# A retention layer and two dense layers on one core: third and fourth head pairs crossed, all loads on one queue, two w_in halves decoded beside the tiles

## The chip, the core and the metric

The kernel runs on one core of one Trainium2 chip. The metric is device time in microseconds (us) from one launch to its end; lower is better. The kernel before takes 866.6 us (median of 3 runs, 865.91 to 866.82).

## What is computed

Three steps follow one another. The reference, cut to what matters:

```python
# q, k, v: (4, 8, 576, 64): 4 batches, 8 heads, 576 positions, 64 wide
gamma = 1.0 - 2.0 ** (-5.0 - np.arange(8))
Dmat = np.where(rel >= 0, gamma[:, None, None] ** rel, 0.0)      # rel = i - j
x = ((q @ k.T) / 8 * Dmat) @ v                                   # -> (2304, 512)
h = x @ w_in;   g = relu(h) ** 2;                x = g @ w_out     # 512 -> 2048 -> 512
h = x @ w_in2;  g = h * clip(h + 3, 0, 6) / 6;   y = g @ w_out2
```

The four weight matrices arrive as 64-bit floats and are decoded to 32 bits on the chip; q, k and v are 32-bit.

## The kernel before

**The tile stage (first 82 us).** The positions of a batch are cut into four tiles of 128 and a last one of 64. There are 20 tiles in the order `tiles`: the tiles of batches 0 and 1 alternate (numbers 0 to 9), then those of batches 2 and 3 (10 to 19). So tiles 8, 9, 18 and 19 are the short last ones, and 0, 1, 10 and 11 the first of their batches. A tile needs two loads: `qkt` (keys and queries, 512 KB) and `kvt` (keys and values by position, 512 KB; in a short tile only the values, 64 rows of 2 KB that are wanted on both halves of the 128 partitions). There are five places for tiles (`TOKENS`), so the loads of tile t+5 wait until tile t is used up. Round ti of the loop issues on TensorE (PE) the scores of tile ti (`aps`), then for tile ti-1 the values (`vps`), the state sums (`sps`) and the queries (`vps` again, none in the first tile of a batch). VectorE (DVE) turns `aps` into `ret`, which `vps` needs, and `vps` into `xall`, the input of the next layer. ScalarE (ACT) copies the state, GpSimd (POOL) scales the keys of a tile (`scale_keys`).

**Weights beside the tiles.** One "half" is a 128-wide slice of one weight matrix, 512 KB as it arrives. `load_w` loads it into a tile `stage`; `decode` makes 32 bits of it in four steps: ACT (`first`), DVE (`clamp`, `second`, `third`). `halves` is the list of the order in which halves are loaded and decoded. Before, the loads number 1 to 7 are issued from ACT's queue, at the places where ACT comes to them, and all others from SP's queue; halves w_in 0, w_in 1 and w_out 0 are decoded between tiles 6 and 11.

**The first layer (82 to 476 us).** It goes over four groups of positions (`FIRST`); within one, 16 units c. A unit is `emit_h` (h = x w_in for 128 of the 2048 columns, banks `hps`), `emit_g` (ACT: relu, square, rounding to `g`; DVE: the remainder) and, two units later (`LAG`), `y_steps` (`yps`, `ytail`). `split_in` and `split_out` cut a decoded half into a high part (ACT copy) and a low part (a subtraction on the engine named) for products of three passes. In the first group `emit_h` writes the same two banks in each unit, so that unit c+1 can start only when ACT has read unit c out (`r<-hps`). Within a unit the engines work in the order of the code: what stands after a waiting instruction on its engine waits too.

**Order of the loads.** SP and ACT issue their loads in the order of the code. The built program has eight completion semaphores for loads and gives them to the loads of both queues in turn, so that each load also waits until the load eight places ahead in the code has landed.

**Crossed pairs.** A head pair a holds heads 2a and 2a+1, which lie on partitions 0 to 63 and 64 to 127. For pairs 1 and 3 `stage_values` writes the two heads to swapped halves, `constants` holds the matching decay (`crossed`), and `load_w` loads the rows of w_in for these two pairs with swapped halves:

## Time and profile before

| what | value |
|---|---|
| median of 3 runs | 866.6 us |
| the profiled execution: its time | 864.64 us |
| the profiled execution: its span, first to last instruction | 862.9 us |
| PE busy | 839.4 us, 97% of the span |
| DVE, ACT, POOL busy | 526.2, 459.5, 138.5 us |
| granted TensorE clock, mean | 0.990 |
| start of the first layer (first `hps`) | 81.65 us |
| chain that ended last | PE 82%, DMA 6%, issue 5%, ACT 3%, POOL 2%, DVE 2% |

The profiled execution took 1.74 us more than its span, and 1.96 us less than the median of the three runs. PE's share of 97% is an average: in the 40 slices of the profile its busy tenths stand at 8777999 in the first seven, and from the eighth on at 9 but for the last. The column PEclk has 8 or 9 in the same first slices.

### The profile page before, as it was taken

The page shows a single profiled execution, that of the slowest core. Times are in us where ns is not written, and L with a number is a line of the kernel's source. Part 1 is how long each engine was busy: PE and PEld are TensorE (multiplying, and loading weights), DVE is VectorE, ACT ScalarE, POOL GpSimd, SP SyncE. Part 2 cuts the span into 40 slices and gives each one's busy share as a digit, 9 for nine tenths or more (in the row PEclk, how much of TensorE's full clock was granted, in tenths as well). Part 3 has the DMA queues.
Part 4 walks back from the last instruction along what each step waited for, and adds up shares of the span by engine and source line. Part 5 has one row for each costly group of instructions (what it writes and reads, how often), then busy time and mean ns, then how long its engine had stood idle before and what let it go on. Part 6 is the DMA issues. An engine that isn't in the chain of part 4 may idle for free.

```text
span 862.9 us, 13373 instructions
## 1 busy us (share of the span) xinstructions
PE 839.4 (97%) x4962; PEld 728.3 (84%) x4962; DVE 526.2 (61%) x896; ACT 459.5 (53%) x878; POOL 138.5 (16%) x117
## 2 busy tenths in 40 slices
PE   8777999999999999999999999999999999999998
PEld 6676888888888888888888898888988988989886
DVE  5575677777476777787675645456554546643433
ACT  2323877677676777787765533335433345433332
POOL 3141333332133313432140000000000000000000
PEclk9889999999999999999999999999999999999999
DMA  9884265655577688778759445545565463774531
GB/s 342 282 302 143 98 187 185 186 196 180 194 288 271 227 285 287 271 266 295 262 202 333 167 159 213 189 151 179 191 268 200 159 217 113 262 259 162 178 115 73
DMA packets 67529, 184.21 MB, mean 213 GB/s; under 512 B 6536, under 2 KB 23048, under 8 KB 67464
## 3 DMA queue, kind: packets, MB, share of 16 engines
q1 hardware_dynamic: 63656, 178.54, 59.0%
q10 hardware_dynamic: 3808, 4.82, 1.7%
q8 instruction: 39, 0.64, 0.3%
q14 instruction: 26, 0.21, 0.1%
HBM read 147.16 MB, written 36.18 MB: 212 GB/s over the span
## 4 chain that ended last, share of the span: by engine, by line
PE 82%; DMA 6%; issue 5%; ACT 3%; POOL 2%; DVE 2%; SPq 0%; ACTq 0%; DVEq 0%; POOLq 0%
PE yps L574 23%; PE hps L608 20%; PE hps L390 18%; PE yps L433 17%; DMA kvt<-in_kv_dram 2%; DMA qkt<-in_qk_dram 2%; DMA stage<-in_w_in_dram 1%; PE ytail L433 1%; POOL win L186 1%; POOL wo L186 1%; PE vps L303 1%; PE aps L255 1%; ACT r L411 0%; DVE ret L263 0%; ACT r L162 0%
## 5 line engine op out<-in xcount | busy, mean ns | idle before, releaser
L574 PE MATMUL yps<-wo,g 128*128 128x512 f32 x864 | 226.3, 394 | 0.0
L433 PE MATMUL yps<-g,wo 128*128 128x512 f32 x768 | 195.7, 392 | 0.6 <-POOL wo L186 0.5
L574 PEld LDWEIGHTS yps<-wo,g 128*128 128x128 f32 x864 | 159.6, 188 | 23.6 <-DVE g L623 0.3
L433 PEld LDWEIGHTS yps<-g,wo 128*128 128x128 f32 x768 | 140.0, 188 | 28.5 <-POOL wo L186 4.1
L390 PE MATMUL hps<-xring,win 128*128 128x512 f32 (+1 forms) x720 | 154.8, 364 | 0.3 <-ACT r L410 0.3
L390 PEld LDWEIGHTS hps<-xring,win 128*128 128x128 f32 x720 | 124.1, 190 | 21.9 <-ACT r L410 0.5
L608 PE MATMUL hps<-xlast,win 128*128 128x384 f32 x576 | 116.1, 336 | 0.0
L608 PEld LDWEIGHTS hps<-xlast,win 128*128 128x128 f32 x576 | 103.2, 188 | 8.8
L627 DVE TENSOR_TENSOR u<-hps,u 128x384 f32<-128x384 f32 x48 | 26.7, 557 | 107.3 <-PE hps L608 107.3
L416 DVE TENSOR_TENSOR g<-r,g 128x512 fp32r<-128x512 f32 x64 | 47.5, 742 | 73.0 <-ACT g L412 72.6
L608 PE MATMUL hps<-xop,win 128*128 128x384 f32 x432 | 87.2, 336 | 0.0
L410 ACT ACTIVATE r<-hps 128x512 f32<-128x512 f32 x80 | 43.9, 549 | 75.9 <-PE hps L390 75.9
L608 PEld LDWEIGHTS hps<-xop,win 128*128 128x128 f32 x432 | 77.5, 188 | 6.6
L621 ACT ACTIVATE g<-c 128x384 fp32r<-128x384 f32 x72 | 37.8, 525 | 84.0 <-DVE c L620 84.0
L619 ACT ACTIVATE v<-c,three 128x384 f32<-128x384 f32 x72 | 44.4, 617 | 32.9 <-DVE c L627 31.7
L390 PE MATMUL hps<-xown,win 128*128 128x512 f32 x240 | 59.8, 390 | 0.7 <-ACT xall L442 0.7
L165 DVE TENSOR_SCALAR a<-a 128x512 f32<-128x512 f32 x64 | 38.5, 601 | 25.6 <-ACT a L161 25.6
L390 PEld LDWEIGHTS hps<-xown,win 128*128 128x128 f32 x240 | 44.8, 188 | 10.1 <-ACT xall L442 0.9
L185 ACT ACTIVATE win<-w 128x512 fp32r<-128x512 f32 x64 | 39.6, 620 | 25.2 <-DVE w L180 23.7
L646 ACT ACTIVATE c<-hps 128x384 f32<-128x384 f32 x24 | 11.8, 492 | 76.7 <-PE hps L608 76.7
L411 ACT ACTIVATE r<-r 128x512 f32<-128x512 f32 x80 | 47.2, 590 | 2.5
L620 DVE SCALAR_TENSOR_TENSOR c<-v,c 128x384 f32<-128x384 f32 x72 | 39.9, 555 | 13.7 <-ACT v L619 13.7
(77 smaller groups left out, 1000.4 us busy)
## 6 DMA issues: line engine op xcount, KB each, us to landing
wo<-kept SPq DMA_DIRECT2D x96, 512.0 KB, 5.3
win<-kept SPq DMA_DIRECT2D x72, 512.0 KB, 3.3
kept<-ready SPq DMA_DIRECT2D x40, 512.0 KB, 3.8
stage<-in_w_out_dram SPq DMA_DIRECT2D x30, 512.0 KB, 4.0
qkt<-in_qk_dram SPq DMA_DIRECT2D x16, 512.0 KB, 8.9
kvt<-in_kv_dram SPq DMA_DIRECT2D x16, 512.0 KB, 8.9
kept<-wo SPq DMA_DIRECT2D x16, 512.0 KB, 5.0
stage<-in_w_in_dram SPq DMA_DIRECT2D x16, 512.0 KB, 3.8
```

What stands on the lines that cost most here:

```text
L165: nc.vector.tensor_scalar(out=a, in0=a, scalar1=LEAST, scalar2=MOST, op0=ALU.max, op1=ALU.min)
L185: nc.scalar.activation(out=hi, in_=src, func=ACTF.Copy)
L390: nc.tensor.matmul(out=h, lhsT=w[:, wp, kk * 128:kk * 128 + 128], rhs=xs[pos, kk][xp][:, o:o + n], start=m == 0, stop=m == 3 * KD - 1,)
L410: nc.scalar.activation(out=r, in_=hs[k], func=ACTF.Relu)
L411: nc.scalar.activation(out=r, in_=r, func=ACTF.Square)
L416: nc.vector.tensor_tensor(out=lo, in0=src, in1=hi.bitcast(F32), op=ALU.subtract)
L433: nc.tensor.matmul(out=p, lhsT=w[:, wp, m * 128:m * 128 + 128], rhs=g[pos, c][k][:, gpart, :size], start=c == 0 and e == 0 and not (k and ...
L574: nc.tensor.matmul(out=p, lhsT=gt[m // 3][:, gpart, m % 3 * 128:][:, :128], rhs=w[:, wp], start=first and e == 0, stop=last and e == 2,)
L608: nc.tensor.matmul(out=to, lhsT=wl[k][:, half, wp, o], rhs=x[:, xp, f], start=first and m == 0, stop=last and m == 5, skip_group_check=True,)
L619: nc.scalar.activation(out=v, in_=c, func=ACTF.Relu, bias=three)
L620: nc.vector.scalar_tensor_tensor(out=c, in0=v, scalar=6.0, in1=c, op0=ALU.min, op1=ALU.mult)
L621: nc.scalar.activation(out=hi, in_=c, func=ACTF.Copy)
```

## The change

1. Pairs 2 and 3 are crossed instead of 1 and 3, and crossed in such a way that the rows of w_in for pair 2's place in `xall` are the 128 consecutive rows 320 to 447. `stage_values` and `stage_queries` write pairs 0 and 1 into one bank and pairs 2 and 3 into the other, and all loops over pairs go in the order 0, 2, 1, 3. The halves that consecutive products write are the same as before.
2. A w_in half comes by four loads (256, 128, 64 and 64 KB) instead of three (256, 128, 128 KB).
3. All halves are loaded from SP's queue; ACT issues none.
4. The values of a short tile come by two loads of 64 partitions instead of one load whose source repeats the rows (`twice`).
5. w_out 0 is no longer decoded beside the tiles. It is decoded in the first unit of the first layer, behind w_in 2, and the low part of its split is done by DVE and no longer by POOL. The two decodes that stay beside the tiles come two tiles later, the splits one tile later or earlier; w_in 0 and w_in 1 are loaded two tiles later.

`AHEAD` is used nowhere.

```diff
@@ constants
-    crossed[:, 1::2] = np.roll(pair, D, axis=0)[:, 1::2]
+    crossed[:64, 2:], crossed[64:, 2] = pair[64:, 2:], pair[:64, 3]
+    crossed[64:, 3] = pair[:64, 2]
@@ load_w
-        queue = nc.scalar if turn["stage"] <= 7 else nc.sync
...
-                queue.dma_start(out=t[:, ::2], in_=src[:, ::2])
-                for e in range(2):
-                    queue.dma_start(out=t[64 * e:64 * e + 64, 1::2], in_=src[64 - 64 * e:128 - 64 * e, 1::2])
+                nc.sync.dma_start(out=t[:, :2], in_=src[:, :2])
+                rows = w_in[:, c * 128:(c + 1) * 128]
+                nc.sync.dma_start(out=t[:, 2], in_=rows[320:448])
+                nc.sync.dma_start(out=t[:64, 3], in_=rows[448:])
+                nc.sync.dma_start(out=t[64:, 3], in_=rows[256:320])
...
-        queue.dma_start(out=t, in_=src)
+        nc.sync.dma_start(out=t, in_=src)
@@ load_kv
-            twice = kv[b, C * i:C * i + n, 1].unsqueeze(0).to_broadcast([2, n, H, D])
-            nc.sync.dma_start(out=kvt[:, 1], in_=twice)
+            for e in range(2):
+                nc.sync.dma_start(out=kvt[half(e), 1], in_=kv[b, C * i:C * i + n, 1])
@@ scale_keys and below
+    PAIRS = (0, 2, 1, 3)
+    def column(a, e):
+        return a % 2 if a < 2 else 1 - (a % 2 ^ e)
@@ stage_values
-        for a in range(HP):
+        for a in PAIRS:
             for e in range(2):
-                to = e ^ a % 2
                 nc.tensor.matmul(
-                    out=p[a % 2][64 * to:64 * to + 64, a // 2, :n],
+                    out=p[a // 2][half(e ^ a // 2), column(a, e), :n],
                     lhsT=kvt[keys(n, e), 1, 2 * a + e, :], rhs=r[keys(n, e), e, a, :n],
-                    start=a < 2, stop=i == 0, skip_group_check=True,
+                    start=a % 2 == 0, stop=i == 0, skip_group_check=True,
@@ halves
-    halves = [(-2, 0, 0, 0), (-2, 0, 1, 0), (-2, 0, 0, 1), (-1, 0, 2, 0)] + sorted(halves, key=lambda x: x[0])
+    halves = [(-2, 0, 0, 0), (-2, 0, 1, 0), (-1, 0, 2, 0), (-1, 0, 0, 1)] + sorted(halves, key=lambda x: x[0])
@@ loop over the tiles
-            if ti in (1, 3, 5) or ti >= len(tiles) - 4:
+            if ti in (3, 5) or ti >= len(tiles) - 5:
                 load()
-            if ti >= 6 and ti % 2 == 0 and halves[0][0] < -1:
+            if ti >= 8 and ti % 2 == 0 and halves[0][0] < -1:
...
-            if ti in (11, 13, 15, 17):
-                split_x(0, (ti - 11) // 2)
-            if ti in (14, 16):
-                split_in(0, (ti - 14) // 2, nc.gpsimd)
+            if ti in (12, 14, 16, 18):
+                split_x(0, (ti - 12) // 2)
+            if ti in (13, 15):
+                split_in(0, (ti - 13) // 2, nc.gpsimd)
@@ first layer
-        due = [decode(*halves.pop(0)[1:])]
-        due[0].pop(0)()
+        due = [decode(*halves.pop(0)[1:]) for _ in range(2)]
+        for d in due:
+            d.pop(0)()
...
-                split_out(max(i - 1, 0), nc.gpsimd)
+                split_out(max(i - 1, 0), nc.vector if i == 0 else nc.gpsimd)
```

**SP's queue around tiles 7 to 10.** These are SP's loads for tiles 7, 8, 9 and the first of tile 10 before; the rows of L227 are the repeated loads of the short tiles 8 and 9.

```order
L217 DMA qkt<-in_qk_dram 128x1024
L224 DMA kvt<-in_kv_dram 128x1024
L217 DMA qkt<-in_qk_last_dram 128x512
L227 DMA kvt<-in_kv_dram 128x1x512
L217 DMA qkt<-in_qk_last_dram 128x512
L227 DMA kvt<-in_kv_dram 128x1x512
L217 DMA qkt<-in_qk_dram 128x1024
```

The same place of the changed kernel, from the second load of tile 7 on:

```order
L226 DMA kvt<-in_kv_dram 128x1024
L135 DMA stage<-in_w_in_dram 128x2x128
L137 DMA stage<-in_w_in_dram 128x128
L138 DMA stage<-in_w_in_dram 64x128
L139 DMA stage<-in_w_in_dram 64x128
L219 DMA qkt<-in_qk_last_dram 128x512
L229 DMA kvt<-in_kv_dram 64x512 x2
L219 DMA qkt<-in_qk_last_dram 128x512
L229 DMA kvt<-in_kv_dram 64x512 x2
L135 DMA stage<-in_w_in_dram 128x2x128
L137 DMA stage<-in_w_in_dram 128x128
```

The loads of w_in 0 have moved in front of tile 8's, those of w_in 1 in front of tile 10's, and each repeated load has become two. The last five halves of the stage stand behind tile 19's loads now.

**ACT's queue in tiles 0 to 5.** Before, ACT's instructions from the first state copies on; L135, L137 and L141 are loads of halves that it issues.

```order
L289 ACTIVATE state<-sps,cst 128x64 x4
L135 DMA stage<-in_w_in_dram 128x2x128
L137 DMA stage<-in_w_in_dram 64x2x128 x2
L289 ACTIVATE state<-sps,cst 128x64 x8
L135 DMA stage<-in_w_in_dram 128x2x128
L137 DMA stage<-in_w_in_dram 64x2x128 x2
L289 ACTIVATE state<-sps,cst 128x64 x8
L141 DMA stage<-in_w_out_dram 128x512
```

In the changed kernel no load stands there: the state copies of tiles 0 to 7 follow one another, and then come the two decodes.

**DVE at the first unit.** Before, from the last `xall` of the tile stage on: the decode of w_in 2 (L165 to L180, its result is `w_1102`), then the remainders of `g`, and then the next decode.

```order
L323 TENSOR_TENSOR xall<-vps,cst 128x2x64 x4
L165 TENSOR_SCALAR a<-a 128x512
L168 TENSOR_SCALAR a<-a 128x512
L174 SCALAR_TENSOR_TENSOR a<-stage,a 128x512
L180 ISA w_1102<-a,r 128x1024
L416 TENSOR_TENSOR g<-r,g 128x512
L416 TENSOR_TENSOR gtail<-r,gtail 128x256
L165 TENSOR_SCALAR a<-a 128x512
```

The same place of the changed kernel; `wd` is the decoded w_out 0 and `wo` its split:

```order
L333 TENSOR_TENSOR xall<-vps,cst 128x2x64 x4
L167 TENSOR_SCALAR a<-a 128x512
L170 TENSOR_SCALAR a<-a 128x512
L176 SCALAR_TENSOR_TENSOR a<-stage,a 128x512
L182 ISA w_1102<-a,r 128x1024
L167 TENSOR_SCALAR a<-a 128x512
L170 TENSOR_SCALAR a<-a 128x512
L424 TENSOR_TENSOR g<-r,g 128x512
L424 TENSOR_TENSOR gtail<-r,gtail 128x256
L176 SCALAR_TENSOR_TENSOR a<-stage,a 128x512
L182 ISA wd<-a,r 128x1024
L188 TENSOR_TENSOR wo<-wd,wo 128x512
```

The second half of w_out 0's decode and the low part of its split now stand behind the remainders of the first unit's `g`. ACT's high part of that split waits for L182 `wd`, and it stands on ACT ahead of the next unit's `r<-hps`.

## Rows read from the trace of the kernel before

**Rows 1.** Windows: stretch, length, busy us (instructions) of PE, PEld, DVE, ACT, POOL, PEclk, DMA share, GB/s.
```profile
8.00:14.00 6.00, 4.80 (x88) 4.35 (x90) 5.22 (x11) 1.31 (x6) 3.13 (x3) 1.00 1.02 411
14.00:24.00 10.00, 8.41 (x170) 7.48 (x170) 5.37 (x11) 2.40 (x11) 2.09 (x2) 1.00 1.04 325
27.50:30.00 2.50, 2.50 (x24) 2.27 (x24) 0.72 (x2) 0.00 (x0) 0.49 (x1) 0.50 1.01 410
37.00:46.00 9.00, 3.27 (x96) 2.97 (x96) 6.41 (x15) 3.17 (x8) 0.00 (x0) 0.88 1.03 324
...
77.50:80.80 3.30, 0.00 (x0) 0.00 (x0) 1.00 (x4) 0.00 (x0) 0.00 (x0) 1.00 0.17 62
...
110.00:200.00 90.00, 89.92 (x511) 77.15 (x510) 67.16 (x105) 67.61 (x129) 30.10 (x22) 1.00 0.61 189
```

**Rows 2.** The chain that ended last, first 82 us: start, length, what.
```profile
21.25 5.81 DMA qkt<-in_qk_dram
...
33.19 13.47 DMA qkt<-in_qk_dram
...
66.66 14.13 DMA kvt<-in_kv_dram
```

**Rows 3.** Timeline of PE: start, length, what, count of matmul records, [idle before and what ended it].
```profile
17.47 1.16 PE L255 MATMUL aps<-qkt 64*128 64x128 f32 x16 [0.73 <-DMA qkt<-in_qk_dram]
...
21.58 1.16 PE L255 MATMUL aps<-qkt 64*128 64x128 f32 x16 [0.86 <-DVE xall L323]
...
27.20 2.08 PE L255 MATMUL aps<-qkt 64*128 64x128 f32 x16 [2.37 <-DMA qkt<-in_qk_dram]
...
33.03 1.41 PE L255 MATMUL aps<-qkt 64*128 64x128 f32 x16
...
46.79 2.08 PE L255 MATMUL aps<-qkt 64*128 64x128 f32 x16 [6.52 <-DMA qkt<-in_qk_dram]
...
55.38 1.16 PE L255 MATMUL aps<-qkt 64*128 64x128 f32 x16
...
62.90 1.16 PE L255 MATMUL aps<-qkt 64*128 64x128 f32 x16
...
66.08 1.16 PE L255 MATMUL aps<-qkt 64*128 64x128 f32 x16
...
80.92 0.46 PE L303 MATMUL vps<-ret,kvt 64*64 64x64 f32 x16 [3.70 <-DMA kvt<-in_kv_dram]
...
81.65 10.08 PE L390 MATMUL hps<-xring,win 128*128 128x512 f32 x48
92.04 4.45 PE L390 MATMUL hps<-xring,win 128*128 128x512 f32 x24 [0.31 <-ACT r L410]
```

**Rows 4.** Timeline of SP's queue: the repeated load of short tile 8.
```profile
25.76 0.69 SPq L227 DMA_DIRECT2D kvt<-in_kv_dram  x1
```

**Rows 5.** Timeline of DVE: tile 19's ret, unit 0's remainder, and two steps of a decode.
```profile
77.18 0.87 DVE L263 TENSOR_TENSOR ret<-aps,decay_last 64x256 f32<-64x256 f32 x2
...
89.35 0.43 DVE L416 TENSOR_TENSOR gtail<-r,gtail 128x256 fp32r<-128x256 f32 x1 [0.48 <-ACT gtail L412]
...
97.37 0.69 DVE L174 SCALAR_TENSOR_TENSOR a<-stage,a 128x512 int32<-128x512 int32 x1
98.20 0.69 DVE L180 CUSTOM_DVE_ANT_0 wd<-a,r 128x1024 uint16<-128x1024 uint16 x1
```

**Rows 6.** Waits of PE in the first 82 us: us in total, times, longest.
```profile
PE vps L303 <- DVE ret L263: 1.3, 3, 0.6
```

**Rows 7.** Timeline of POOL: the scaling of tile 3's keys, started by its load.
```profile
14.77 1.05 POOL L240 TENSOR_TENSOR kvt<-kvt,cst 128x512 f32<-128x512 f32 x1 [1.60 <-DMA kvt<-in_kv_dram]
```

**Rows 8.** Timeline of ACT: read-out of units 0 and 1, and between them w_out 0's split.
```profile
86.16 0.60 ACT L410 ACTIVATE r<-hps 128x512 f32<-128x512 f32 x1 [2.39 <-PE hps L390]
...
89.75 0.61 ACT L185 ACTIVATE wo<-wd 128x512 fp32r<-128x512 f32 x1
...
91.41 0.57 ACT L410 ACTIVATE r<-hps 128x512 f32<-128x512 f32 x1
```

More of the change, by code (lines that the diff above doesn't have):

```diff
@@ L36 @@
 LAG = 2
-AHEAD = 3
+AHEAD = 2
 WARM = 18
@@ L242, in scale_keys, with half @@
         )
+    def half(i):
+        return slice(64 * i, 64 * i + 64)
     def keys(n, e):
-        return slice(0, n) if n == C else slice(64 * e, 64 * e + 64)
+        return slice(0, n) if n == C else half(e)
+    PAIRS = (0, 2, 1, 3)
+    def column(a, e):
+        return a % 2 if a < 2 else 1 - (a % 2 ^ e)
     def stage_scores(ti):
@@ L256, in stage_scores @@
                     out=pe[e][keys(n, e), a, :n],
-                    lhsT=qkt[64 * e:64 * e + 64, 0, a, :n],
-                    rhs=qkt[64 * e:64 * e + 64, 1, a, :n],
+                    lhsT=qkt[half(e), 0, a, :n],
+                    rhs=qkt[half(e), 1, a, :n],
                     start=True, stop=True,
@@ L298, in stage_values @@
         p = [next_bank([128, 4, C], "vps") for j in range(2)]
-        for a in range(HP):
+        for a in PAIRS:
             for e in range(2):
-                to = e ^ a % 2
                 nc.tensor.matmul(
-                    out=p[a % 2][64 * to:64 * to + 64, a // 2, :n],
+                    out=p[a // 2][half(e ^ a // 2), column(a, e), :n],
                     lhsT=kvt[keys(n, e), 1, 2 * a + e, :], rhs=r[keys(n, e), e, a, :n],
-                    start=a < 2, stop=i == 0, skip_group_check=True,
+                    start=a % 2 == 0, stop=i == 0, skip_group_check=True,
                 )
@@ L312, in stage_queries @@
         qkt = data.pop(ti)[0]
-        for a in range(HP if i else 0):
+        for a in PAIRS if i else ():
             for e in range(2):
-                own, to = slice(64 * e, 64 * e + 64), e ^ a % 2
                 nc.tensor.matmul(
-                    out=p[a % 2][64 * to:64 * to + 64, a // 2, :n],
-                    lhsT=states[b % 2][i % 2][own, a, :], rhs=qkt[own, 1, a, :n],
+                    out=p[a // 2][half(e ^ a // 2), column(a, e), :n],
+                    lhsT=states[b % 2][i % 2][half(e), a, :], rhs=qkt[half(e), 1, a, :n],
                     start=False, stop=True, skip_group_check=True,
@@ L322, in stage_queries @@
         for j in range(2):
-            nc.vector.tensor_tensor(
-                out=xall[:, j::2, t:t + n], in0=p[j][:, :2, :n], in1=gq[:, j::2, :n], op=ALU.mult
-            )
+            own = slice(2 * j, 2 * j + 2)
+            nc.vector.tensor_tensor(out=xall[:, own, t:t + n], in0=p[j][:, :2, :n], in1=gq[:, own, :n], op=ALU.mult)
     def parts(pos):
```

## The prediction

> **What bounds the kernel now.** I read the windows first [rows 1]. From 110 us on PE is busy 89.92 of 90.00 us at full clock (2.4 GHz): behind the first units nothing is to be won, and the change moves nothing there but loads. All of the gain or loss must come from the tile stage and the first units. In the tile stage the chain of waits [rows 2] shows three long transfers as the last thing waited for: 5.81, 13.47 and 14.13 us. The timeline of PE [rows 3] says what they cost: PE stands idle 2.37 us before tile 6, 6.52 us before tile 10 and 3.70 us before the values of tile 19.
>
> The timeline also shows a second cost. At full clock one tile takes PE 66.08 - 62.90 = 3.18 us; tile 6, right behind its wait, takes 33.03 - 27.20 = 5.83 us, since its products run at half the pace (2.08 us instead of 1.16 for the scores): the granted clock from 27.50 to 30.00 is 0.50, that is 1.2 GHz [rows 1]. The same 2.08 stands behind the wait of 6.52. Behind the wait of 3.70 the first two units of the first layer take 10.08 us, where the next unit alone takes 4.45. Waits of 0.73 and 0.86 us were followed by 1.16, so the clock stayed up there.
>
> Why are the loads late? 14.13 us is the load of a short tile that repeats its rows: 256 KB. While PE waits for it (77.50 to 80.80) the DMA engines are busy for 0.17 of their time and move 62 GB/s, whereas 8 to 14 us shows 411 GB/s at a share of 1.02 [rows 1]. So it isn't the bandwidth that is short; the load keeps only a few of the 16 DMA engines at work. Its sisters of tiles 8 and 9 are issued around 25.76 us [rows 4], and the `qkt` issued behind them at 33.19 lands after 13.47 us, at 46.66; PE goes on at 46.79. My reading: a load is complete when its last engine is, and the few engines that carry the repeated loads hold back every load behind them. The waits of 0.73, 0.86 and 2.37 us lie where ACT's queue loads w_in beside SP's tiles: 14 to 24 us moved 325 GB/s only, at a full share.
>
> **The change, part by part.**
>
> *Values of the short tiles by two loads* (source 64 rows, destination 64 partitions). Each should spread over the engines as the w_in loads of 64 partitions do. Then the two long transfers fall to the pace of the others, and this goes: the 6.52 us wait; the half clock behind it, of which I count the one row, 2.08 - 1.16 = 0.92; and of the wait of 3.70 us what isn't hidden by the next thing that is late, tile 19's `ret` on DVE, which ends at 77.18 + 0.87 = 78.05 [rows 5], so that 80.92 - 78.12 = 2.80 us are won. Sum 10.24 us.
>
> *One queue, w_in two tiles later.* Loads now come one behind the other. The waits of 0.73 and 0.86 us and the 2.37 us should go, and with the last its half clock: 5.83 - 3.18 = 2.65, and 1.41 - 1.16 = 0.25 in the next scores. Sum 6.86 us. The row of 0.86 names DVE's `xall`; the six banks come free three allocations earlier than that, so I count it as a load. If I am wrong, 0.86 stays. What is late next is the load stream itself. Tile 3's keys and values are there at 14.77 [rows 7]. From then to the `qkt` of tile 13, 9.96 MB have to land (tiles 4 to 7 and 10 to 12 at 1.049 MB, two short tiles and two w_in halves at 0.524 each, one qkt of 0.524). At 411 GB/s that is 24.2 us, so 39.0. PE now reaches tile 13 at 55.38 [rows 3]; less the waits and half clocks counted so far before it (2.37 + 6.52 + 2.90 + 0.92 + 0.73 + 0.86 = 14.30) that is 41.1. So the stream stays ahead, by 2 us. At 325 GB/s, the rate of the two stretches with trouble [rows 1], it would be 45.4, and PE would wait 4.3 us in all. Both of these stretches have a cause that the change takes away, so I take 411 and keep 325 for a bound.
>
> The Trainium skill ("DMA: Bandwidth & Descriptors", Specifications) gives one core about 358 GB/s of HBM bandwidth. By that limit the 9.96 MB would take an estimated 27.8 us, land at 42.6 and cost 1.5 us; this case's 411 GB/s [rows 1] does not bear the limit out.
>
> *Crossing.* As many products of the same shapes, whose destination halves alternate as before; the DVE products have the same size. Nothing, either way. *Four loads for a w_in half:* one more issue on SP, 0.69 us by the nearest row [rows 4]. In the first layer the halves are loaded three ahead of their decode and PE is busy 89.92 of 90, so this is hidden; if all 11 extra ones lay bare (w_in 5 to 15), it would be 7.6 us.
>
> *Two decodes instead of three beside the tiles, two tiles later.* They now stand beside tiles 8 to 11, where the short tiles give PE little work, and DVE does a tile's `ret` behind a decode's steps (0.69 us each, [rows 5]). The nearest row is DVE's `ret` as a wait of PE: 1.3 us in three waits [rows 6]. I add as much again, 1.3 us; bounds 0 and 3.0, two pairs of decode steps (98.20 + 0.69 - 97.37 = 1.52) quite uncovered.
>
> *w_out 0 decoded in the first unit.* Unit 2 starts when ACT has read unit 1 out; that is now 0.31 us late [rows 3]. Before: from unit 0's read-out at 86.16 to unit 1's at 91.41, 5.25 us [rows 8]. Now DVE finishes the remainder at 89.35 + 0.43 = 89.78, 3.62 behind 86.16; then two steps of w_out 0's decode follow, 1.52; then ACT's copy of w_out 0, which waited for them, and from that copy to unit 1's read-out 91.41 - 89.75 = 1.66. Together 6.80: 1.55 us later. Against it, units 0 and 1 lose their half clock, 10.08 - 2 x 4.45 = 1.18, since no wait of 3.70 stands before them. Net +0.37. Bounds: -1.18 if the decode is done sooner and the 1.55 doesn't show; +2.90 more if the wait before unit 2, which then comes to about 2 us, brings the half clock as the one of 2.37 did. It lies between 0.86, which did not, and 2.37, which did; I take none. POOL loses this subtraction, which nobody waits for.
>
> **Sum.** -10.24 - 6.86 + 1.3 + 0.37 = -15.43 us. The profiled execution took 864.64 (span 862.9 and 1.74 around it): 849.2. The median of runs is 1.96 above it: **851.2 us**. Own range of this case: 848 (no wait on DVE, no late read-out) to 857 (3.0 on DVE, half clock before unit 2, the 0.86 stays).
>
> **Rivals.**
>
> *The stream is slower than PE* (0.17). 4.3 us of waits by 325 GB/s, and behind one of them the half clock of 2.90: 851.2 + 7.2 = 858.4. For it: a share of 1.0 at 324 GB/s for 9 us [rows 1]; packets of 1 and 2 KB, of which there are now more. Against it: 411 with one queue at work.
>
> *The two loads are no quicker than the one* (0.06). Then the 10.24 us stay, and 866.6 - 6.86 + 1.67 = 861.4. Here stands a rule that speaks against the change: the Trainium skill ("DMA: Bandwidth & Descriptors", Rules for kernel authors) says that two transfers to disjoint halves of the partitions gain nothing over one of 128 partitions, because both run on the same 16 engines. The one transfer of this trace did not run on them all (0.17), and the same section says that a leading broadcast of c copies keeps a load to c engines, here 2 of 16 or 0.125, which fits that row.
>
> *One queue blocks itself: slower* (0.05). Each load waits for the one eight places ahead, and SP issues in order. Between tiles 7 and 10 there now stand 14 small loads in a row (2 x 4 of w_in, 6 of the short tiles), 2.1 MB, 5.1 us at 411 GB/s. A load took 5.81 us from issue to landing in the chain [rows 2]; with eight in flight 14 of them take 10.2 us, 5.1 more than their bytes. It decides against the change from the point where they take 20.5 us, that is with fewer than four in flight; with two, 40.7 us, it would end near 887. Against it: with 64 KB the small ones land sooner than the 512 KB of that row.
>
> *Gains and losses cancel within 0.2%*, about what a measurement of this kernel can tell from no change (0.04): the loads are quicker, but the first units wait for weights until the old 82 us.
>
> The forecast has 0.68. Faster by over 0.2%: 0.68 + 0.17 + 0.06 = 0.91; within: 0.04; slower: 0.05. The range goes from 847, a little below the own range since nothing in the stage need wait, to 859, which takes in the slow stream and leaves out the other three, 0.15, and a little at either end.
>
> **What the profile will show.** Right: the first `hps` at about 65.9 us instead of 81.65; no transfer over 9 us in the chain of the stage; no wait of PE over 2 us in it, and PEclk at 1.00 from 10 us on; the share of DMA near 1 and about 400 GB/s whenever loads are pending. Units 0 and 1 take 8.9 us together, and unit 2 starts some 10.4 us behind the first `hps`, with ACT's read-out as the releaser and the copy of w_out 0 waiting for DVE. From 30 us behind the first `hps` on, the trace is that of before, moved. Wrong: `kvt` of tiles 8, 9, 18, 19 still landing last; PE waiting for `qkt` of tiles 10 to 13 (the slow stream); a DMA share far below 1 while SP waits for the load eight places ahead (the blocked queue); or half clock in the stage without a wait, which none of my terms has.

## The result, and the profile after

The changed kernel takes 853.4 us (median of four runs, 852.17 to 855.22) against 866.36 us before (865.91 to 866.82): a ratio of 0.9852, 95% interval 0.9831 to 0.9873. The forecast was 851.2 us. The profiled execution took 854.20 us (span 852.4) where the sum had 849.2, so the mechanism must be judged by 5.0 us, not by the 2.2 us between the medians: the profiled execution of before lay 1.96 us below its median, that of after 0.8 above.

Where the time came from shows on TensorE. This is the timeline of PE after the change (start, length, what, matmul records, idle time before and what ended it): the scores of tiles 10, 11 and 13, the values of tile 19, units 0 and 1 together, and unit 2.

```profile
36.17 2.08 PE L266 MATMUL aps<-qkt 64*128 64x128 f32 x16 [2.87 <-DMA qkt<-in_qk_dram]
...
40.03 2.08 PE L266 MATMUL aps<-qkt 64*128 64x128 f32 x16 [0.72 <-DVE xall L333]
...
47.92 1.16 PE L266 MATMUL aps<-qkt 64*128 64x128 f32 x16
...
69.57 0.86 PE L313 MATMUL vps<-ret,kvt 64*64 64x64 f32 x13 [1.62 <-DVE ret L274]
...
70.65 8.66 PE L398 MATMUL hps<-xring,win 128*128 128x512 f32 x48
...
81.96 4.45 PE L398 MATMUL hps<-xring,win 128*128 128x512 f32 x24 [2.65 <-ACT r L418]
```

The first step-1 products (`hps`) start at 70.65 us instead of 81.65 [rows 3]: 11.0 us won, where 15.8 were forecast. From there to the end it is 852.4 - 70.65 = 781.75 us, before 862.9 - 81.65 = 781.25: 0.5 lost, where 0.37 was to be lost by the forecast. So nearly the whole miss of 5 us lies in the tile stage. The waits of 6.52 us before tile 10 and of 3.70 us for tile 19's load are gone, and so are the 2.37 us before tile 6. But tile 10 waits again, 2.87 us, for the same kind of load, and behind it the scores take 2.08 us instead of 1.16: the half clock (1.2 GHz, PEclk 0.50) is back.

The waits of PE in the first 100 us (us in total, times, longest) say the same. `aps<-DMA qkt` is the load stream, `hps<-ACT r` the late read-out of unit 1, `vps<-DVE ret` tile 19.

```profile
PE aps L266 <- DMA qkt<-in_qk_dram: 4.2, 3, 2.9
PE hps L398 <- ACT r L418: 2.7, 1, 2.7
PE vps L313 <- DVE ret L274: 1.8, 2, 1.6
PE aps L266 <- DVE xall L333: 1.3, 2, 0.7
```

The chain that ended last (start, length, what) now has two transfers in the stage instead of 5.81, 13.47 and 14.13 us [rows 2]: the start, and tile 10's.

```profile
2.68 7.87 DMA qkt<-in_qk_dram
...
31.46 4.58 DMA qkt<-in_qk_dram
```

A transfer of 4.58 us is a quick one. It is late because it was issued late. Tile 10 takes the place of tile 5, with which PE had done at 26.68 us; its load was issued at 31.46, 4.8 us later. The windows show what the stream did in the meantime (columns as in [rows 1]; the last three are PEclk, share of the DMA engines, GB/s):

```profile
10.00:15.00 5.00, 4.32 (x76) 4.04 (x78) 3.58 (x7) 1.75 (x8) 1.98 (x3) 1.00 1.02 411
...
20.00:25.00 5.00, 5.00 (x100) 4.35 (x94) 3.18 (x7) 1.63 (x8) 2.09 (x2) 1.00 1.04 390
25.00:30.00 5.00, 5.00 (x120) 4.57 (x118) 3.07 (x7) 1.57 (x8) 1.04 (x1) 1.00 0.80 208
30.00:35.00 5.00, 3.31 (x108) 3.03 (x102) 3.66 (x10) 2.34 (x8) 0.00 (x0) 1.00 0.96 265
35.00:40.00 5.00, 3.14 (x48) 2.75 (x48) 3.62 (x10) 1.26 (x2) 1.04 (x1) 0.57 0.98 329
40.00:45.00 5.00, 4.97 (x50) 4.66 (x52) 3.35 (x7) 0.03 (x1) 1.42 (x2) 0.50 1.03 412
```

Up to 25 us, one queue moves about 400 GB/s, as the forecast had it. From 25 to 35 us it moves 208 and 265. In this stretch stand the 14 small loads (two w_in halves and two short tiles). Two things are short there: at a share of 0.80 the engines partly have nothing to do, and even at 0.96 they move 265 and not 411, so the bytes of these loads cost more time each.

SP's queue goes with the first of these. From the first small load (17.45) to 27.95 us SP stands still between the small loads, each time for a load eight places ahead that has not landed. There are eight such waits, 6.8 us together, among them (us in total, times, longest):

```profile
SPq L219 <- DMA kvt<-in_kv_dram: 1.3, 1, 1.3
SPq L229 <- DMA stage<-in_w_in_dram: 1.0, 1, 1.0
SPq L138 <- DMA qkt<-in_qk_dram: 0.9, 1, 0.9
```

From 27.95 us on SP issues without a pause, about half a microsecond for each small load, and tile 10's comes behind the last one.

```profile
29.11 0.58 SPq L135 DMA_DIRECT2D stage<-in_w_in_dram  x1
...
30.77 0.59 SPq L139 DMA_DIRECT2D stage<-in_w_in_dram  x1
31.46 0.54 SPq L219 DMA_DIRECT2D qkt<-in_qk_dram  x1
```

Two smaller losses lie on DVE. Before tile 19's `ret` (69.11) now stands the low part of the last operand split (68.23), and the last step of w_out 0's decode (77.98) takes 1.67 us, where the same step took 0.69 [rows 5].

```profile
68.23 0.96 DVE L188 TENSOR_TENSOR xring<-xall,xring 128x768 fp32r<-128x768 f32 x1 [0.41 <-ACT xring L187]
69.11 0.87 DVE L274 TENSOR_TENSOR ret<-aps,decay_last 64x256 f32<-64x256 f32 x2
...
77.98 1.67 DVE L182 CUSTOM_DVE_ANT_0 wd<-a,r 128x1024 uint16<-128x1024 uint16 x1
```

POOL's timeline has a split running beside that step:

```profile
77.49 1.61 POOL L188 TENSOR_TENSOR win<-w,win 128x512 fp32r<-128x512 f32 x1 [17.03 <-ACT win L187]
```

and ACT's timeline the consequence, the read-outs of unit 0 (73.74) and unit 1 (81.34) with w_out 0's split between them, waiting for DVE:

```profile
73.74 0.60 ACT L418 ACTIVATE r<-hps 128x512 f32<-128x512 f32 x1 [3.32 <-PE hps L398]
...
79.68 0.63 ACT L187 ACTIVATE wo<-wd 128x512 fp32r<-128x512 f32 x1 [2.27 <-DVE wd L182]
...
81.34 0.57 ACT L418 ACTIVATE r<-hps 128x512 f32<-128x512 f32 x1
```

The two read-outs are 7.60 us apart; before 5.25 [rows 8], forecast 6.80.

### The profile page after: what moved, and what is told of

Read it like the earlier page. It is cut to its first block, busy times and chain, and to the rows that moved or that the text cites. A ratio compares the mean times of both kernels' runs of the same rounds, so it can differ in the third digit from the quotient of the medians.

```text
span 852.4 us, 13413 instructions
## 1 busy us (share of the span) xinstructions
PE 836.3 (98%) x4962; PEld 725.8 (85%) x4962; DVE 527.6 (62%) x897; ACT 459.2 (54%) x878; POOL 136.9 (16%) x116
## 4 chain that ended last, share of the span: by engine, by line
PE 94%; ACT 2%; DMA 1%; DVE 1%; issue 1%; POOL 0%; SPq 0%; ACTq 0%; DVEq 0%
PE yps L582 24%; PE hps L398 22%; PE hps L616 21%; PE yps L441 20%; PE ytail L441 2%; PE aps L266 2%; PE vps L313 2%; DMA qkt<-in_qk_dram 1%; PE sps L289 1%; PE vps L325 1%; DVE ret L274 0%; ACT r L419 0%; ACT r L418 0%; ACT a L163 0%; ACT state L300 0%
```

## The experiments

All times are medians; the ratio is to the kernel before on the same chip. The changed kernel's own is 0.9852. Where two kernels of different batches are compared, the ratios are the safer measure.

**Two loads alone.** The kernel before, with only the short tiles' values loaded twice:

```diff
-            twice = kv[b, C * i:C * i + n, 1].unsqueeze(0).to_broadcast([2, n, H, D])
-            nc.sync.dma_start(out=kvt[:, 1], in_=twice)
+            for e in range(2):
+                nc.sync.dma_start(out=kvt[64 * e:64 * e + 64, 1], in_=kv[b, C * i:C * i + n, 1])
```

> The kernel before, with only the values of the short tiles by two loads. Theory F (the load that repeats its rows runs on a few of the 16 DMA engines and holds back all behind it): the wait of 6.52 us before tile 10 falls under 1, that of 3.70 before tile 19's values under 1; the 2.37 us before tile 6 with its half clock stays. Time 866.4 - 10.2 = 856 (853 to 859). Rival (two halves are no quicker than one load; the gain came from the single queue): 866, and 6.52 stays.

Measured: 855.44 us (853.75 to 858.33), ratio 0.9877 [0.9851, 0.9904]: 10.9 us less than the 866.3 beside it. PE's timeline (as above) keeps the wait before tile 6. The waits of 6.52 us before tile 10 and of 3.70 us for tile 19's load are gone, and a wait for DVE's `ret` with half clock behind it has come:

```profile
27.16 2.08 PE L255 MATMUL aps<-qkt 64*128 64x128 f32 x16 [2.42 <-DMA qkt<-in_qk_dram]
...
45.68 0.43 PE L303 MATMUL vps<-ret,kvt 128*64 128x128 f32 x2 [1.58 <-DVE ret L263]
...
48.18 2.08 PE L255 MATMUL aps<-qkt 64*128 64x128 f32 x16
...
75.19 9.88 PE L390 MATMUL hps<-xring,win 128*128 128x512 f32 x48
```

So the medians bear the term of 10.24 us out, and this one edit carries most of the whole gain. The rival that two loads are no quicker than one is dead. The trace shows less: it is of the slowest of the four executions, 858.33 us, only 6.3 below the 864.64 of before. Waits for DVE's `ret`, 1.58 us the longest, and half clock take back the rest there, and units 0 and 1 take 9.88 us, although PE waited no longer than 0.58 us at a time in the 20 us before them.

**The repeated load put back** into the changed kernel (the diff above, reversed).

> The changed kernel with the repeated load put back. Theory F: tile 10 waits 6 us or more instead of 2.87 and tile 19's values 3 or more, the share of DMA falls to about 0.13 to 0.2 in the second of these waits; 853.4 + 6 to 11 = 860 to 864. Rival: within 1 us of 853.4.

Measured: 861.34 us (860.57 to 862.1), ratio 0.9939 [0.9922, 0.9956]. Both waits of before return. The first is longer than it was, though tile 10 starts sooner (42.32 us, before 46.79), since PE comes to it sooner still (42.32 - 7.85 = 34.47 us, before 40.27):

```profile
42.32 2.08 PE L266 MATMUL aps<-qkt 64*128 64x128 f32 x16 [7.85 <-DMA qkt<-in_qk_dram]
...
74.75 0.71 PE L313 MATMUL vps<-ret,kvt 64*64 64x64 f32 x16 [4.08 <-DMA kvt<-in_kv_dram]
```

One expectation failed: the share of DMA does not fall to 0.13 to 0.2 in the second wait. From 71.0 to 74.5 us it is 0.62, at 185 GB/s. The halves of the weights now stand behind tile 19's load in the same queue, and they keep moving while PE waits, until SP itself, from 70.15 us on, has to wait for the load eight places ahead, tile 19's. In the kernel before, a repeated load can be seen nearly by itself from 66 to 67 us, when tile 18's, issued at 63.48, is still under way (columns as in [rows 1]):

```profile
66.00:67.00 1.00, 1.00 (x24) 0.92 (x16) 0.76 (x2) 1.00 (x4) 0.72 (x1) 1.00 0.13 49
```

A share of 0.13 is that of two engines out of 16.

**One queue alone.** The kernel before, with all halves on SP's queue:

```diff
-        queue = nc.scalar if turn["stage"] <= 7 else nc.sync
+        queue = nc.sync
```

> The kernel before, with only the queue changed: all halves on SP's queue. By my sum the 2.37 us before tile 6, its half clock of 2.90, and 0.73 and 0.86 go, the waits behind the repeated loads stay: 866.4 - 6.9 = 859.5 (857 to 863). Rival A (the two w_in halves, now ahead of the tiles in the same queue, only move the wait): 864 to 868. Rival B (the queue blocks itself): over 868.

Measured: 863.89 us (862.5 to 865.0), ratio 0.9969 [0.996, 0.9979]: 2.4 us, where 6.9 were expected. The timeline of PE tells where the rest went. The wait before tile 6 falls to 1.08 us and its half clock goes, but tile 10, behind the repeated loads, waits 8.83 us instead of 6.52:

```profile
24.61 1.16 PE L255 MATMUL aps<-qkt 64*128 64x128 f32 x16 [1.08 <-DMA qkt<-in_qk_dram]
...
46.30 2.08 PE L255 MATMUL aps<-qkt 64*128 64x128 f32 x16 [8.83 <-DMA qkt<-in_qk_dram]
```

PE comes to tile 10 at 37.47 us instead of 40.27, but starts it at 46.30 instead of 46.79: time won before a wait for a load with a fixed arrival is given back at that load. The two edits are worth 10.9 and 2.4 us alone; the whole change is worth 13.0.

**The old crossing** in the changed kernel: pairs 1 and 3 crossed, a w_in half by three loads.

```diff
...
-                nc.sync.dma_start(out=t[:, :2], in_=src[:, :2])
-                rows = w_in[:, c * 128:(c + 1) * 128]
...
+                nc.sync.dma_start(out=t[:, ::2], in_=src[:, ::2])
+                for e in range(2):
+                    nc.sync.dma_start(out=t[64 * e:64 * e + 64, 1::2], in_=src[64 - 64 * e:128 - 64 * e, 1::2])
...
-    PAIRS = (0, 2, 1, 3)
+    PAIRS = (0, 1, 2, 3)
...
```

> The changed kernel with the crossing of before: second and fourth head pairs crossed, a w_in half by three loads (one over 128 partitions, two over 64) instead of four. The theory that the new crossing is worth nothing on TensorE and that the four loads are hidden: first step-1 products and time as in the changed kernel, 852.5 to 854.5 us, the wait before tile 10 between 2 and 3 us and three issues instead of four in each half. If the number of small loads is what makes tile 10 wait, two fewer of them ahead of it bring its load about 1 us earlier: 852 us. Rival: the loads over 64 partitions, each now with two rows of the half, are slower than the four, tile 10 waits over 3.5 us and the time is 855 us or more.

Measured: 853.98 us (851.86 to 856.21), ratio 0.9867 [0.9847, 0.9887]; tile 10 waits 2.72 us, without half clock behind it in the profiled execution, which is the quickest of the four. The new crossing and the fourth load are worth nothing that can be measured, as the prediction had it. Two small loads fewer ahead of tile 10 bring nothing either: its load was issued at 30.92 and took 5.7 us, so it landed at 36.6, in the changed kernel at 31.46 + 4.58 = 36.04.

**No crossing at all**, and so one load of 512 KB for a w_in half:

```diff
-    crossed[:64, 2:], crossed[64:, 2] = pair[64:, 2:], pair[:64, 3]
-    crossed[64:, 3] = pair[:64, 2]
...
-        return a % 2 if a < 2 else 1 - (a % 2 ^ e)
+        return a % 2
...
-                    out=p[a // 2][half(e ^ a // 2), column(a, e), :n],
+                    out=p[a // 2][half(e), column(a, e), :n],
...
```

> The changed kernel with no pair crossed and each w_in half by one load of 512 KB: 14 loads between tiles 7 and 10 become 8, of the same bytes. Theory N (the number of small loads holds the stream back: each waits for the one eight places ahead): tile 10's wait of 2.87 us falls under 1, the half clock of tiles 10 to 12 goes, 853.4 - 6.5 = 847 (845 to 850), if the uncrossed products take as long. Rival (bytes and 1 KB rows do it): 2 to 3 us of wait stay, 853. Rival on the crossing itself: products that follow one another on the same rows and columns of the array cost more; each 0.1 us on a tile's 3.18 would be 2 us in all.

Measured: 854.2 us (852.72 to 854.94), ratio 0.9857 [0.9842, 0.9873], no different from the changed kernel, by two effects of opposite sign. The granted clock of its four runs is 0.998 to 1.000 (0.990 to 0.994 in the changed kernel), and the timeline of PE shows tile 10's scores at 35.56 with no wait:

```profile
35.56 1.16 PE L257 MATMUL aps<-qkt 64*128 64x128 f32 x16
```

By the DMA view its load, issued at 27.98, took 6.1 us and landed at 34.1, 1.9 us sooner than in the changed kernel. It went out 0.3 us after its place was free, not 4.8: 8 loads of the same bytes in the place of 14 hold the queue up far less, and the share from 25 to 30 us is 1.08, not 0.80. But PE also comes later: it reaches tile 10 at 35.56, in the changed kernel at 33.30 (36.17 - 2.87), since its own work is slower here. Groups of PE's instructions between 46 and 69 us (busy us, mean ns): this kernel, then the changed one.

```profile
L316 PE MATMUL vps<-qkt,state 64*64 64x128 f32 x96 | 6.5, 275 | 0.0
```

```profile
L325 PE MATMUL vps<-qkt,state 64*64 64x128 f32 x96 | 4.0, 282 | 0.0
```

The same 96 query products take 6.5 us without a crossing and 4.0 with it. There are 192 of them in the stage: 5 us. So the crossing, old or new, is worth about 5 us on PE, and since the times are equal, the small loads that it forces cost about as much in this order of the loads. The expectation had named PE's side as a condition and as a rival, with 0.1 us on a tile; a tile takes 3.60 us here instead of 3.18.

**w_in later.** The loads of w_in 0 and 1 behind the loads of tiles 12 and 14, and their decodes with them (the expectations count these tiles one too high: 13 and 15 here, 15 and 17 in the last experiment):

```diff
-            if ti in (3, 5) or ti >= len(tiles) - 5:
+            if ti in (8, 10) or ti >= len(tiles) - 5:
...
-            if ti >= 8 and ti % 2 == 0 and halves[0][0] < -1:
+            if ti >= 12 and ti % 2 == 0 and halves[0][0] < -1:
...
-            if ti in (12, 14, 16, 18):
-                split_x(0, (ti - 12) // 2)
+            if ti in (10, 11, 16, 17):
+                split_x(0, ti % 2 + ti // 16 * 2)
...
```

> The changed kernel with w_in 0 and 1 loaded later in the one queue: their eight loads stand behind the loads of tiles 13 and 15 instead of ahead of those of tiles 9 and 11, their decodes move to tiles 12 to 15, and two operand splits and both w_in splits move with them. Theory of order (the small loads are slow as a group and, standing ahead of tile 10's query-key load, make TensorE wait 2.87 us there, after which it runs at half clock until tile 13): the 2.87 and most of the 3.84 us of half clock go, tile 10 starts at about 33.3 us, the first step-1 products at about 64 to 65 us, median 846 to 848 us. Rival of VectorE (it is full enough beside tiles 12 to 19 that the decodes there make TensorE wait for ret or xall as much as the loads did): a wait for DVE of 1 to 3 us in tiles 13 to 19 and 850 to 853 us. Rival of the stream (all loads ahead of tile 10 are simply too many bytes): not possible here, since fewer bytes are ahead; if the wait before tile 10 stays above 2 us the small loads had nothing to do with it.

Measured: 850.68 us (849.05 to 851.0), ratio 0.9821 [0.9804, 0.9837]; less won than expected. Tile 10's load, issued at 26.71, took 5.1 us and landed at 31.8, 4.2 us sooner than in the changed kernel, and PE no longer waited for it. The half clock between tiles 10 and 13 is gone. But PE's timeline has the wait at tiles 13 and 15, the first tiles behind the small loads in their new place, and half clock in unit 2:

```profile
43.43 1.16 PE L266 MATMUL aps<-qkt 64*128 64x128 f32 x16 [2.02 <-DMA qkt<-in_qk_dram]
...
51.32 1.16 PE L266 MATMUL aps<-qkt 64*128 64x128 f32 x16 [1.47 <-DMA qkt<-in_qk_dram]
...
67.49 8.63 PE L398 MATMUL hps<-xring,win 128*128 128x512 f32 x48
...
78.78 6.04 PE L398 MATMUL hps<-xring,win 128*128 128x512 f32 x24 [2.66 <-ACT r L418]
```

Order decides where the wait is, and DVE is not what replaces it. Here tile 10's load waits for its place alone: PE had done with tile 5 at 26.63 us. The arrivals also measure the small loads: the same 1.05 MB of w_in ahead of tile 10 delay its load by 4.2 us as eight loads, and by 34.1 - 31.8 = 2.3 us as the two loads without a crossing, of which 1.0 us is PE's, which frees the place later there (27.66 us).

**w_out 0 back beside the tiles**, decoded from tiles 8, 10 and 13 on with the two w_in halves:

```diff
...
-            if ti in (3, 5) or ti >= len(tiles) - 5:
+            if ti in (3, 5, 7) or ti >= len(tiles) - 4:
...
-            if ti >= 8 and ti % 2 == 0 and halves[0][0] < -1:
+            if ti in (8, 10, 13) and halves[0][0] < -1:
...
-        due = [decode(*halves.pop(0)[1:]) for _ in range(2)]
+        due = [decode(*halves.pop(0)[1:])]
...
```

The low part of w_out 0's split is POOL's again.

> The changed kernel with w_out 0 decoded beside the tiles as before the change (its load third, behind tile 12's loads, decodes from tiles 8, 10 and 13; its low part again on GpSimd). Theory of the decode in unit 0 (the wait of 2.65 us before unit 2 is the price of w_out 0 being decoded between the read-outs of units 0 and 1): that wait falls to under 0.5 us and unit 2 starts some 8.9 to 9.1 us after the first step-1 products; VectorE has 2.2 us more to do beside the tiles, which may cost up to 1 us there: 850.5 to 852.5 us. Rival (the later units have slack that takes up what unit 2 loses, or the pace of the loads moves the loss elsewhere): the wait goes but the time stays at 853 to 854.5 us.

Measured: 853.36 us (851.86 to 853.74), ratio 0.9855 [0.984, 0.9869]: no different. The wait before unit 2 is gone, as the theory said, but PE's timeline shows the price beside the tiles, a wait for DVE's decode (`a`) among it:

```profile
35.69 1.16 PE L266 MATMUL aps<-qkt 64*128 64x128 f32 x16 [2.33 <-DVE xall L333]
...
39.64 1.16 PE L266 MATMUL aps<-qkt 64*128 64x128 f32 x16 [2.16 <-DVE a L170]
...
79.44 4.45 PE L398 MATMUL hps<-xring,win 128*128 128x512 f32 x24 [0.29 <-ACT r L418]
```

So the part of the change that moves w_out 0's decode into unit 0 is worth nothing that shows against this place for it: it trades one wait for another.

**w_out 0's split one unit later:**

```diff
-            if i <= NCH and i != 1:
-                split_out(max(i - 1, 0), nc.vector if i == 0 else nc.gpsimd)
+            if 1 <= i <= NCH:
+                split_out(i - 1, nc.gpsimd)
```

> The changed kernel with one step moved: w_out 0's split stands in unit 1, behind w_in's, with its low part on GpSimd, instead of in unit 0 with its low part on VectorE. The wait of 2.65 us before unit 2 is for ScalarE's read-out of unit 1, which stands behind this split's high part at 79.68 us, and that waits 2.27 us for VectorE's last decode step (1.67 us beside GpSimd's split, 0.69 us elsewhere). Theory: ScalarE is free for the read-out from about 78.9 us, unit 1's products end at about 79.3 us, so the wait falls from 2.65 to about 0.6 us and the median to 851.3 us (850.8 to 852). Rival (work queued behind moves into unit 1 and y of unit 0 waits for its low part, or unit 3 waits for its read-out): the wait appears before y of unit 0 or before unit 3 with 1 to 2.5 us, 853 to 854 us.

Measured: 850.34 us (849.16 to 851.78), ratio 0.9824 [0.9807, 0.984]. Units 0 to 2 run without a gap (72 records in one row). The rival's wait appears too, 1.54 us before y of unit 0 where the changed kernel has 0.30, so that 2.65 - 1.24 = 1.4 us are won here:

```profile
68.76 12.85 PE L398 MATMUL hps<-xring,win 128*128 128x512 f32 x72
83.65 0.50 PE L441 MATMUL yps<-g,wo 128*128 128x512 f32 x1 [1.54 <-POOL wo L188]
```

The median fell by 3 us, more than that; the intervals of the two ratios overlap a little, and the rest is not accounted for. In the profiled execution the first `hps` came at 68.76 us, 1.9 sooner than in the changed kernel's, in a stage that this edit does not touch.

**Operand splits one tile earlier:**

```diff
-            if ti in (12, 14, 16, 18):
-                split_x(0, (ti - 12) // 2)
-            if ti in (13, 15):
-                split_in(0, (ti - 13) // 2, nc.gpsimd)
+            if ti in (11, 13, 15, 17):
+                split_x(0, (ti - 11) // 2)
+            if ti in (12, 14):
+                split_in(0, (ti - 12) // 2, nc.gpsimd)
```

> The changed kernel with the four operand splits one tile earlier (beside tiles 11, 13, 15 and 17 instead of 12, 14, 16 and 18) and the two w_in splits at tiles 12 and 14. VectorE's 0.96 us for the last split's low part no longer stands ahead of tile 19's ret: theory, the wait of 1.62 us before tile 19's values falls to about 0.7 us and the first step-1 products come 0.9 us sooner, 852.5 us (852 to 853.2). Rival: the split now delays tile 18's ret by as much, or ScalarE's and VectorE's decode ahead of unit 0 sets the start anyway: 853.2 to 854.

Measured: 851.27 us (849.41 to 851.96), ratio 0.983 [0.9814, 0.9846]. Tile 19's wait falls by 1.2 us, to

```profile
65.08 0.85 PE L313 MATMUL vps<-ret,kvt 64*64 64x64 f32 x13 [0.42 <-DVE ret L274]
```

which is this edit's part. The median fell by 2.1 us, more than expected, but the intervals of the two ratios overlap. The profiled execution also had no half clock behind the wait before tile 10 (2.54 us there); nothing shows that this is the edit's doing.

**Two combinations**: both small moves (w_out 0's split one unit later and the operand splits one tile earlier), and w_in later with w_out 0's split one unit later. The edits are those shown.

> The changed kernel with both small moves: the four operand splits one tile earlier (851.27 us alone) and w_out 0's split behind unit 1's w_in split (850.34 us alone). The two waits lie in different stages (tile 19, unit 2): the gains of 2.1 and 3.0 us add to 848.3 us (847.5 to 849.5); the wait before tile 10 stays at 2.5 to 2.9 us. Rival: unit 0's start, earlier by 1 us, runs into its decodes or into y's wait for w_out 0 (1.54 us in the single run), so that only 3 to 4 us are left: 849.5 to 850.5.

> The changed kernel with the w_in loads and decodes later (as in the run with w_in later, 850.68 us) and w_out 0's split moved behind unit 1's w_in split (850.34 us alone). If the two gains are of different waits they add, less the 1.6 us of half clock that the first one's profile has in unit 2: 2.7 + 3.0 us below 853.4, 847.5 us (846.5 to 848.5), no wait before unit 2, waits of 1.5 to 2 us before tiles 12 and 14 as before. Rival: the loads of w_in 2 and w_out 0, now behind more, come late for unit 0 and 1: 849 to 851.

Measured: 850.11 us (849.02 to 851.07), ratio 0.9814 [0.9798, 0.9829], and 850.09 us (847.81 to 850.2), ratio 0.9814 [0.9797, 0.9832]. Neither adds up as expected. (The waits before tiles 12 and 14 that the expectations name here and below are those before 13 and 15.) The time of the first is where its rival put it, 849.5 to 850.5. Its trace, of the slowest of its executions, shows more than the rival's wait of 1.54 us before y of unit 0: tile 10 waits 3.02 us, tile 11 another 2.02, and half clock follows. The second was profiled in its quickest execution (847.81, as expected), and the other three took 850.0 to 850.2 at a granted clock of 0.998 to 1.000; they left no trace, so what they lost stays open.

**w_in later still**, behind the loads of tiles 14 and 16, with w_out 0's split one unit later as above:

```diff
-            if ti in (3, 5) or ti >= len(tiles) - 5:
+            if ti in (10, 12) or ti >= len(tiles) - 5:
...
-            if ti >= 8 and ti % 2 == 0 and halves[0][0] < -1:
+            if ti >= 14 and ti % 2 == 0 and halves[0][0] < -1:
...
-            if ti in (12, 14, 16, 18):
-                split_x(0, (ti - 12) // 2)
-            if ti in (13, 15):
-                split_in(0, (ti - 13) // 2, nc.gpsimd)
+            if 10 <= ti < 14:
+                split_x(0, ti - 10)
+            if ti in (16, 18):
+                split_in(0, (ti - 16) // 2, nc.gpsimd)
...
```

> The changed kernel with w_in 0 and 1 loaded behind the loads of tiles 15 and 17, decoded at tiles 14 to 17, operand splits at tiles 10 to 13, w_in splits at tiles 16 and 18, and w_out 0's split behind unit 1's w_in split. If small loads in the stream while TensorE is close behind it are what costs, the waits before tiles 10, 12 and 14 all go or stay under 1 us, the first step-1 products come at 64.5 to 66 us and the median is 845.5 us (844.5 to 847). Rival: the stream from 25 to 35 us is slowed by the short tiles' own loads, so that tiles 10 to 14 wait 1 us or more without any small w_in load ahead; or VectorE, with a decode beside tiles 14 to 17, makes TensorE wait there: 847 to 849 us.

Measured: 847.41 us (846.65 to 847.83), ratio 0.9782 [0.9766, 0.9797], the best of all and clear of the changed kernel's interval. It is 0.4 us above the expected range, where the rival lies, but the rival's waits are not in the trace, and the first `hps` came when expected. All four runs have a granted clock of 1.000. PE's timeline from 11 us to unit 0 has no wait over 0.81 us; these are the last one for a load, tile 19's, the first units, and y of unit 0:

```profile
55.97 0.68 PE L266 MATMUL aps<-qkt 64*128 64x128 f32 x7 [0.62 <-DMA qkt<-in_qk_dram]
...
64.01 0.85 PE L313 MATMUL vps<-ret,kvt 64*64 64x64 f32 x13 [0.42 <-DVE ret L274]
65.09 12.85 PE L398 MATMUL hps<-xring,win 128*128 128x512 f32 x72
79.98 0.50 PE L441 MATMUL yps<-g,wo 128*128 128x512 f32 x1 [1.54 <-POOL wo L188]
```

The windows still show a slower stream where the short tiles' six loads stand, but SP isn't held up by it: from 16 to 33 us nearly all that its tile loads wait for is PE, which has to free their places.

```profile
25.00:30.00 5.00, 5.00 (x121) 4.50 (x116) 3.06 (x8) 1.85 (x8) 1.04 (x1) 1.00 0.98 273
```

```profile
SPq L219 <- PE vps L325: 12.3, 6, 2.8
```

## Why the prediction was right, and where it was off

- **Two loads for the short tiles, -10.24.** Right by the medians: -10.9 alone, -7.9 seen from the changed kernel; in the one profiled execution of the edit alone, 6.3. The reading of [rows 1, 2], a load on few engines that holds back those behind it, stands. The Trainium skill ("DMA: Bandwidth & Descriptors", Rules for kernel authors) says that two transfers of half the partitions gain nothing over one of 128. Here they won 10.9 us over one transfer that repeated its rows, by itself at a share of 0.13. The same section of the Trainium skill says that a leading broadcast of c copies confines a load to at most c engines; with two copies that share agrees.
- **One queue, -6.86.** Right as far as tile 10 for the whole change: PE is ready for it at 36.17 - 2.87 = 33.30 us, and the sum has 46.79 - 2.37 - 6.52 - 2.90 - 0.73 - 0.86 = 33.41. Alone it is worth 2.4 us, because of the repeated load behind it.
- **"So the stream stays ahead, by 2 us."** This step failed, and with it three signs: no wait of PE over 2 us, PEclk at 1.00, and about 400 GB/s. It took 411 GB/s throughout and a queue that nothing holds up, on the ground that both stretches with 325 had a cause that the change takes away. The 14 small loads are a new cause: 208 and 265 GB/s from 25 to 35 us, SP held up for 6.8 us by loads eight places ahead, and tile 10's load issued 4.8 us after its place was free. PE reaches tile 13 at 47.92 us instead of 41.1: 2.87 us of wait for tile 10's load, 0.72 before tile 11, and for the rest half clock (11.75 us from tile 10 to 13 with 0.72 of wait in them, against 7.7 in the sum). That is the size that the slow-stream rival had, 4.3 + 2.90 = 7.2 us, and its place. The mechanism is at least as much that of the rival of the queue that blocks itself, whose signs are there (a share of 0.80 while SP waits for the load eight places ahead), at a small part of its price. That rival worked out 5.1 us more than the bytes for the 14 loads with eight in flight, and the sum left this out. Against the margin of 2 us it would have made a wait of about 3.1 us; 2.87 were measured. This agreement was found afterwards, and how much is due to dearer bytes and how much to the held queue was not separated. That the median still came within 2.2 us is luck: 2.0 us of other terms in the stage came out better (below), and the profiled executions stand differently to their medians by 2.76 us (1.96 below, 0.80 above).
- **Decodes beside tiles 8 to 11, +1.3.** Too much: before tile 19 DVE's `ret` made PE wait only 0.16 us in the stage, unless the 0.72 us before tile 11, put down to DVE's `xall`, is counted. **Tile 19, 2.80 of 3.70.** Too much by 0.72: 1.62 us remain instead of 0.90, since the change puts an operand split ahead of that `ret`, a move that the prediction's working passed over. Splits one tile earlier cut it to 0.42. Of the rest from tile 13 to the first `hps`, PE took 22.73 us; 26.27 - 2.80 = 23.47 were in the sum.
- **w_out 0's decode, +0.37.** Unit 2 starts 81.96 - 70.65 = 11.31 us behind the first `hps`, not 10.76 as by the sum (the 10.4 among the signs leaves the 0.37 out). The read-outs lie 0.80 us further apart than worked out, and one row covers that: the last decode step took 1.67 us beside POOL's split instead of 0.69. The wait that followed, 2.65 us where about 2 was put, did not bring half clock in this execution (4.45); the same wait did in three experiments (6.03 and 6.04). The bound of +2.90 was right to be kept. Units 0 and 1 lost their half clock as forecast (8.66 us), but the two loads alone left it there (9.88 us) with the wait of 3.70 us gone, so the reason given for it is not the whole one.
- **Crossing and four loads, 0.** Right by the old crossing in the changed kernel.
- **The rest of the trace moved.** Right within 0.5 us.

The sum in one line: 65.85 us for the first `hps`, + 6.84 at tile 13, - 1.3 that DVE didn't cost, - 0.74 behind tile 13, makes 70.65. With w_in's loads behind those of tiles 14 and 16 the first `hps` comes at 65.09: what the prediction had for the stage could be had, in another order of loads.

## What to carry to other kernels

A load that occupies few DMA engines costs more than its own time, since the loads behind it in the same queue end later too; look for transfers of over 10 us beside a low share of the DMA engines. When all loads share a queue, a forecast needs a rate for each stretch by what stands there (here 411 GB/s with large loads, 208 to 265 with 14 small ones). Where a load must also wait for the one eight places ahead, count loads as well as bytes. Small loads that aren't urgent belong where the consumer is far behind the stream. And a wait of a few microseconds is worth more than itself when half clock may follow, so take out the cause of the longest wait before shaving the others, and don't add gains of edits whose waits lie in front of the same load.

## What the runs showed that was not expected

The order of the destination halves is worth about 5 us: 96 query products of 64 rows take 4.0 us when consecutive pairs cross their halves and 6.5 when all go straight, with the same shapes and banks. Why is open.

DVE's last decode step, with two operands, took 1.31 to 1.67 us wherever an instruction of POOL was running as it began, in all 14 traces, and 0.69 otherwise. Without a crossing it began at 37.77 us, before POOL's scaling of keys at 38.00; it took 0.69 there, and POOL's scaling 1.36 instead of 1.04. The Trainium skill ("SBUF — State Buffer", SBUF: two separate sides) says that VectorE with two SBUF inputs and GpSimd share a port pair as an exclusive lock; the rows agree with that, and no run here measures it alone.

The length of a wait did not decide whether half clock followed. Behind 2.87 us before tile 10 in the changed kernel it did; behind 2.72 with the old crossing and 2.54 with the splits one tile earlier, at the same place, it did not; behind 1.58 us with the two loads alone it did.
